# One row-sum matmul set for two attention heads, with the weights folded to 64 rows by DMA

## The chip, the cores and the metric

The kernel runs on one core of one Trainium2 chip. The metric is the device time of one execution in microseconds (us). Three executions of the kernel before took 1892.85, 1893.73 and 1894.67 us; the median, 1893.73 us, is the time that the change is measured against.

## The reference

The output is a gated mix of two blocks that read the same input `x` (2048 tokens of 1024 numbers, all in float32):

```python
g = sigmoid((x * gate_w).sum(-1, keepdims=True))
a = mha(x, wqkv, wo)             # 32 heads of 32 dimensions
b = peer(x, w_q, k1, k2, u, v)   # per token and head: best of 64 experts, gelu, weighted sum
out = g * a + (1 - g) * b

# inside mha, for each head:
scores = q @ k.T * 32 ** -0.5    # 2048 x 2048
p = softmax(scores, axis=-1)
o = p @ v                        # 2048 x 32
```

The change touches the denominators of the softmax. The kernel keeps the exponentials unnormalised, multiplies them with `v`, sums them over the keys, and divides at the end.

## The kernel before

**Stages.** First come the projections to `q` and `k`, the router of the experts, and the values `v`, stored to DRAM in two halves of 16 heads. Then comes the attention stage, head after head, about half of the time, and last the multiplication with `wo` and the output.

**Value stage.** `values(ts, half)` (L550) computes token tiles of 128 rows, 24 matmuls each, into one PSUM bank per tile. `bank()` (L99) hands out eight banks in turn, and `values_out` (L561) copies a bank to SBUF on ACT and stores it. The last four tiles of the first half are computed together (`fin0`, L626), with the weights' inner index as the outer loop, so that the weights of the second half can take their places one after the other. Then the first four tiles of the second half are computed in the same way, in banks 0 to 3, because L637 rounds the counter up to a multiple of eight. Just before `fin0` runs the tile of tokens 11, and before that `peer_turn` (L604), whose four copies on ACT each wait for a store from one shared buffer.

**Attention stage.** The 2048 x 2048 weights of a head are made transposed: keys on the 128 partitions, queries along the free dimension. One head has 16 key tiles `kt`. The loop at L875 takes two key tiles per turn; I call this a pair, and a head has pairs 0 to 7. In a turn TensorE (PE) first computes eight score matmuls of this pair (L714), each into one of the seven banks of `ring`. ScalarE (ACT) turns them into exponentials `P` of 128 x 2048 numbers per key tile (L724). Then PE multiplies the exponentials of the pair before with the values (`pv`, L735, four matmuls side by side on 32 columns each). Then the turn issues what `at(step, ...)` has put down for its two steps (a step is one key tile; a head has 16). On PE, ACT, VectorE (DVE) and the DMA queues everything runs in the order in which it is issued here.

**Row sums.** The 16 tiles `P` of a head have to be summed over all keys. `presum` (L752) splits this: tile 1 is written straight into a tile `accd`; tiles 3, 8 and 12 are added to `accd` by DMAs on the GpSimd (POOL) queue that add to what is there; each of these waits for the one before, since all three write `accd`. The other tiles are added on DVE into `acc`. At step 5 of the next head `merge` (L765) adds `accd` to `acc` on DVE; at step 8 `head_sums` (L768) takes one bank of the ring and multiplies the 128 x 2048 result with a 128 x 32 tile of ones, four matmuls side by side (L748). I call these four a set. ACT copies the bank out (`norm_sums`, L781, tile `ssb`), and the SyncE (SP) queue stores one row of every 32 to DRAM (`smd`). For every four heads, `load_r` and `norm_r` (steps 10 and 14 of the next head) load the sums, take reciprocals, multiply with the gate and store them.

**Buffers.** `P` has eight slots (pool `pp`, L661), used in turn by the 15 tiles of a head that are not `accd`. So the slot of tile 3 comes back at tile 11 of the same head, that of tile 8 at tile 0 of the next head, and that of tile 12 at tile 5 of the next head. A slot is free when both `pv` and the adder (DVE or the DMA) have read it. `acc` and `accd` have two buffers each. `finish` (L774, step 0 of the next head) copies the head's output out on ACT and stores it (`od`), and right behind it in SP's order (step 2) stand the seven loads of K and Q of the head after (`load_head`, 1.5 MB), and at step 7 a load of values (`V`).

**Loads for the end.** `wo` (4 MB) lies in one tile `wo_raw`, loaded in 16 pieces at step 11 of heads 8 to 23. `v_raw`, `AT`, the first chunk of outputs and its reciprocals follow in heads 28 to 31.

Of the kernel before, what the change touches and what calls it, by code (L numbers as in the profile page):

```python
# [30 lines left out]
def gated_mha_peer_kernel(ctx, tc, xT, wqkv, wv, wo, wq, k12, ug, v, out):  # L31
# [29 lines left out]
    nc.vector.memset(ones, 1.0)  # L61
    G64 = const.tile([128, 64], F32, name="G64")
# [3 lines left out]
    const.tile([128, 56], F32, name="fill")  # L66
# [553 lines left out]
    for t in range(4, NT - 4):  # L620
        values_out(*values([t], 0))
        if t == 5:
            Ahl = peer_act()
        if t == 10:
            peer_turn(Ahl)
    fin0 = values(list(range(NT - 4, NT)), 0)  # L626
# [10 lines left out]
    bank_no[0] += -bank_no[0] % 8  # L637
# [16 lines left out]
    wo_raw = keep.tile([128, KC, D], F32, name="wo_raw")  # L654
# [90 lines left out]
    def rowsum(ps, *srcs):  # L745
        for src in srcs:
            for qc in range(NQ):
                yield nc.tensor.matmul(ps[32 * qc:32 * qc + 32, :], ones,  # L748
                                       src[:, qc * 512:(qc + 1) * 512],
                                       start=(src is srcs[0]), stop=(src is srcs[-1]))  # L750
# [17 lines left out]
    def head_sums(h):  # L768
        i, = ring_banks(1)
        for ins in rowsum(ring[:, i, :], ACC.pop(h)):  # L770
            on_ring(ins, i)
        on_ring(norm_sums(h, ring[:, i, :]), i)
# [8 lines left out]
    def norm_sums(h, ps):  # L781
        g, j = divmod(h, 4)
        o = wk.tile([128, 512], F32, name="ssb")
        ins = nc.scalar.activation(o, ps, AF.Copy)
        dma(SMD[g][j:j + 1, :].rearrange("o (q s) -> (o q) s", q=NQ), o[::32, :])
        return ins
# [36 lines left out]
    def split_first(step):  # L823
        o = OC[0][:, 0, :]
        if step == 0:
            W0.append(zp.tile([128, 2, D], F32R, name="z1"))
            OH[0] = zp.tile([128, KC, W], F32R, name="z0")
            OL[0] = wk.tile([128, KC, W], F32R, name="acc")
            nc.vector.tensor_mul(o, o, RB[0][:, 0, :])
        elif step == 1:  # L830
            nc.scalar.activation(W0[0][:, 0], wo_raw[:, 0, :], AF.Copy)
        elif step == 2:
            nc.scalar.activation(OH[0][:, 0, :], o, AF.Copy)
        else:
            for lo, src, hi in ((W0[0][:, 1], wo_raw[:, 0, :], W0[0][:, 0]),
                                (OL[0][:, 0, :], o, OH[0][:, 0, :])):
                nc.vector.tensor_tensor(out=lo, in0=src, in1=hi.bitcast(F32), op=OP.subtract)
# [6 lines left out]
    for h in range(H):  # L844
        base = h * NT
        g, j = divmod(h, 4)
        if h < H - 1:
            at(base + NT, finish, h)
            at(base + NT + 5, merge, h)
            at(base + NT + 8, head_sums, h)  # L850
        if j == 3 and g + 1 < G:
            at(base + NT + 10, load_r, g)
            at(base + NT + 14, norm_r, g)
# [7 lines left out]
    for k in range(2 * KC):  # L861
        c = slice(k * D // 2, (k + 1) * D // 2)
        at((8 + k) * NT + 11, dma, wo_raw.rearrange("p k m -> p (k m)")[:, c], wo[:, c])
# [85 lines left out]
    def split_hi(kc):  # L949
        nc.scalar.activation(woh[kc], wo_raw[:, kc, :], AF.Copy)  # L950
# [5 lines left out]
    def split_lo(kc):  # L956
        nc.vector.tensor_tensor(out=wol[kc], in0=wo_raw[:, kc, :],
# [25 lines left out]
    split(woh[0], wol[0], wo_raw[:, 0, :])  # L983
# [67 lines left out]
```

## Time and profile before

| what | value |
|---|---|
| median of three executions | 1893.73 us (1892.85 to 1894.67) |
| the profiled execution | 1894.6 us, of which the span from the first to the last instruction is 1892.8 us |
| granted TensorE clock, mean | 0.998 |
| PE, ACT, DVE busy | 1875.8, 1158.7, 1202.2 us |
| attention stage | from about 667 to 1695 us of the span |
| DMA | 302.72 MB, mean 160 GB/s |

A line of the page's groups gives line, engine, operation, tiles (out<-in), shapes and count, then the busy time in us, the mean of one in ns, the idle time of the engine just before them, and what ended it. In a timeline the columns are start, duration, engine, line, operation, tiles and count; in brackets stands the idle time before the first, and what ended it. PEld is the loading of weights, SPq a DMA issued by SyncE. In a table by windows the columns are the window, its length, the busy time of PE, PEld, DVE, ACT and POOL with the number of instructions, the granted clock, the DMA engines' share and GB/s. A matmul's duration is its latency; matmuls overlap, so their spacing is read from the starts.

### The profile page before, as it was taken

How to read it: one execution, taken by the hardware profiler on the slowest of the kernel's cores; microseconds unless marked ns; L12 is line 12 of the kernel's file. 1: busy time of each engine (PE TensorE's matmuls, PEld its weight loads, DVE VectorE, ACT ScalarE, POOL GpSimd, SP SyncE). 2: the span in 40 equal slices, each digit the busy share in tenths (PEclk: the TensorE clock that was granted, in tenths of full speed). 3: DMA queues.
4: the chain of work that ended last, by engine and by line, in shares of the span. 5: the costliest groups of instructions: out<-in, count | busy, mean ns of one | idle time of the engine just before them, and what ended most of it. 6: DMA issues, size and time to landing. Idle time of an engine off the chain costs nothing.

```text
span 1892.8 us, 25742 instructions
## 1 busy us (share of the span) xinstructions
PE 1875.8 (99%) x10271; PEld 1157.9 (61%) x10271; DVE 1202.2 (64%) x916; ACT 1158.7 (61%) x1413; POOL 148.6 (8%) x183
## 2 busy tenths in 40 slices
PE   9999999999998999999999999999999999999999
PEld 7877777887887844444444444444444444448887
DVE  4522224866520068888888888888888888895220
ACT  4211111200121189999999999999999999993110
POOL 0000000035200000000000000000000000010000
PEclk9999999999999999999999999999999999999999
DMA  5777774420222167777777776877777777756521
GB/s 211 278 270 254 264 271 137 137 73 2 79 88 79 46 161 166 160 172 159 175 169 183 167 184 157 184 162 184 170 176 170 164 166 179 188 128 172 154 89 67
DMA packets 108082, 302.72 MB, mean 160 GB/s; under 512 B 14724, under 2 KB 48660, under 8 KB 84472
## 3 DMA queue, kind: packets, MB, share of 16 engines
q1 hardware_dynamic: 70520, 154.76, 27.4%
q0 software_dynamic: 14976, 103.29, 26.3%
q10 hardware_dynamic: 22464, 43.00, 7.0%
q8 instruction: 81, 1.33, 0.3%
q14 instruction: 41, 0.34, 0.1%
HBM read 138.73 MB, written 62.66 MB: 106 GB/s over the span
## 4 chain that ended last, share of the span: by engine, by line
PE 76%; ACT 0%; DMA 0%; ACTq 0%; issue 0%; DVE 0%
PE ring L714 28%; PE o L735 25%; PE pa L918 9%; PE bk L558 9%; PE bk L401 2%; PE ring L748 1%; PE pa L927 1%; PE o L558 0%; ACT P L724 0%; PE o L748 0%; ACT vo L564 0%; DMA vd<-vo 0%; PE bk L608 0%; ACT accd L724 0%; ACTq L71 0%
## 5 line engine op out<-in xcount | busy, mean ns | idle before, releaser
L724 ACT ACTIVATE P<-ring 128x512 f32<-128x512 f32 (+2 forms) x1034 | 914.5, 984 | 14.9 <-PE o L735 1.4
L763 DVE TENSOR_TENSOR acc<-acc,P 128x2048 f32<-128x2048 f32 x319 | 730.9, 2291 | 74.1 <-ACT P L724 48.8
L735 PE MATMUL o<-P,V 128*32 128x512 f32 x3840 | 464.8, 599 | 0.0
L714 PE MATMUL ring<-z,z 98*128 98x512 f32 x1024 | 272.0, 407 | 1.3 <-ACT P L724 0.8
L714 PE MATMUL ring<-Q,K 98*128 98x512 f32 x1024 | 272.0, 407 | 0.9 <-ACT P L724 0.9
L714 PEld LDWEIGHTS ring<-Q,K 98*128 98x128 f32 x1024 | 182.0, 188 | 145.1 <-ACT P L724 75.1
L714 PEld LDWEIGHTS ring<-z,z 98*128 98x128 f32 x1024 | 182.1, 188 | 144.1 <-ACT P L724 75.1
L735 PEld LDWEIGHTS o<-P,V 128*32 128x32 f32 x3840 | 98.8, 109 | 223.2 <-issue 214.1
L89 ACT ACTIVATE hi<-bk 128x512 fp32r<-128x512 f32 x64 | 37.6, 598 | 242.6 <-PE bk L325 226.9
L325 PE MATMUL bk<-xh,whi 128*128 128x512 f32 x448 | 176.2, 393 | 0.1
L325 PE MATMUL bk<-xh,wlo 128*128 128x512 f32 x448 | 174.4, 389 | 0.0
L325 PE MATMUL bk<-xl,whi 128*128 128x512 f32 x448 | 174.4, 389 | 0.0
L757 POOL DMA_DIRECT2D accd<-P x95 | 81.5, 858 | 1104.8 <-ACT P L724 521.4
L90 DVE TENSOR_TENSOR lo<-bk,hi 128x512 fp32r<-128x512 f32 x64 | 44.1, 689 | 187.5 <-ACT hi L89 183.0
L761 DVE TENSOR_TENSOR acc<-P 128x2048 f32<-128x2048 f32 x32 | 73.4, 2293 | 77.2 <-ACT P L724 77.2
L558 PE MATMUL bk<-wvh,xh 128*128 128x512 f32 x248 | 97.6, 393 | 4.9 <-ACT vo L564 4.9
L325 PEld LDWEIGHTS bk<-xh,whi 128*128 128x128 f32 x448 | 84.1, 188 | 24.1 <-issue 6.7
L558 PE MATMUL bk<-wvl,xh 128*128 128x512 f32 x248 | 97.0, 391 | 0.0
L558 PE MATMUL bk<-wvh,xl 128*128 128x512 f32 x248 | 97.0, 391 | 0.0
L325 PEld LDWEIGHTS bk<-xh,wlo 128*128 128x128 f32 x448 | 84.1, 188 | 17.8
L325 PEld LDWEIGHTS bk<-xl,whi 128*128 128x128 f32 x448 | 84.1, 188 | 16.9
L564 ACT ACTIVATE vo<-bk 128x512 f32<-128x512 f32 x31 | 18.5, 597 | 115.6 <-PE bk L558 109.7
(163 smaller groups left out, 1662.4 us busy)
## 6 DMA issues: line engine op xcount, KB each, us to landing
accd<-P POOLq DMA_DIRECT2D x95, 1024.0 KB, 7.5
wqt<-in_wq SPq DMA_DIRECT2D x32, 1024.0 KB
vd<-vo ACTq DMA_DIRECT2D x32, 256.0 KB
z<-kdh SPq DMA_DIRECT2D x32, 256.0 KB
z<-qdh SPq DMA_DIRECT2D x32, 256.0 KB
V<-vd SPq DMA_DIRECT2D x32, 256.0 KB
K<-kdh SPq DMA_DIRECT2D x32, 256.0 KB
Q<-qdh SPq DMA_DIRECT2D x32, 256.0 KB
```

Source lines behind the costliest of these rows:

```text
L89: nc.scalar.activation(hi, src, AF.Copy)
L90: (on or nc.vector).tensor_tensor(out=lo, in0=src, in1=hi.bitcast(F32), op=OP.subtract)
L325: nc.tensor.matmul(ps, a[:, kc, :], b[:, kc, n * 512:(n + 1) * 512], start=first, stop=last)
L401: nc.tensor.matmul(ps, a[:, kc, tok], b, start=first, stop=last)
L558: nc.tensor.matmul(p, a[:, kc, tok], b, start=first, stop=last)
L714: on_ring(nc.tensor.matmul(ring[:, i, :], K[:98, kt * 128:(kt + 1) * 128], Q[:98, qc * 512:(qc + 1) * 512], start=True, stop=True), i)
L724: on_ring(nc.scalar.activation(P[h, kt][:, q0 * 512:(q0 + m) * 512].rearrange("p (a m) -> p a m", a=m), ring[:, i:i + m, :], AF.Exp, scale ...
L735: nc.tensor.matmul(O[h][32 * qc:32 * qc + 32, :], Vt[g][:, kt, 32 * j:32 * j + 32], p[:, qc * 512:(qc + 1) * 512], start=(kt == 0), stop=( ...
L757: nc.gpsimd.dma_start(ACCD[h], P[h, kt], accum_op=OP.add)
L761: nc.vector.tensor_add(ACC[h], P[h, 0], P[h, kt])
L763: nc.vector.tensor_add(ACC[h], ACC[h], P[h, kt])
L918: nc.tensor.matmul(pa[tt, half], a[:, kc, tt * 128:(tt + 1) * 128], b[:, half * 512:(half + 1) * 512], start=(first and kc == kcs[0] and i ...
```

## The change

- **One set for two heads.** A second weight tile `ones2` has ones in rows 0 to 63 of columns 0 to 15 and in rows 64 to 127 of columns 16 to 31, zeros elsewhere. A tile `T` of 128 x 2048 holds the even head's weights in its upper 64 rows and the odd head's in its lower 64. One set gives the sums of both heads.
- **Folding.** For an even head, DVE adds `acc` and `accd` into `T`, and a DMA on the POOL queue adds the lower 64 rows of `T` to the upper ones. For an odd head, DVE adds the upper 64 rows of `accd` to those of `acc`, then writes the sum of the lower rows to the lower half of `T`, and a DMA adds the upper rows of `acc` to it. Both stand at step 5 of the next head, where `merge` stood.
- **When.** The common set stands at step 15 of the head after the odd one, for heads 0 to 29 (15 sets for 30 heads). Heads 30 and 31 stay as they were. `norm_sums` issues one store for each head. `load_r` and `norm_r` move from steps 10 and 14 to 18 and 22 after the group's last head, that is, to steps 2 and 6 of the head after the next; at step 2 `load_r` is issued ahead of `load_head`.
- **wo.** `wo_raw` becomes two tiles of 2 MB. `T` is the first half of the second one. The first tile is loaded in heads 8 to 15 as before; the four 512 KB pieces of the second are loaded at step 15 of head 30 and steps 3, 6 and 9 of head 31. `v_raw`, `AT`, the first chunk and its reciprocals move one to two heads ahead.
- **Value banks.** The counter is now set to bank 4 ahead of `fin0`, and is no longer rounded behind it: `fin0` takes banks 4 to 7, and the second half's first four tiles take 0 to 3 as before.

```diff
+    ones2 = const.tile([128, 32], F32, name="ones2")
+    nc.vector.memset(ones2, 0.0)
+    for i in range(2):
+        nc.vector.memset(ones2[64 * i:64 * i + 64, 16 * i:16 * i + 16], 1.0)
-    const.tile([128, 56], F32, name="fill")
+    const.tile([128, 24], F32, name="fill")
...
+    bank_no[0] += (4 - bank_no[0]) % 8
     fin0 = values(list(range(NT - 4, NT)), 0)
...
     values_out(*fin0)
-    bank_no[0] += -bank_no[0] % 8
     values_out(*values(list(range(4)), 1))
...
-    wo_raw = keep.tile([128, KC, D], F32, name="wo_raw")
+    wo_raw = [keep.tile([128, KC // 2, D], F32, name=f"wo_raw{i}") for i in range(2)]
+
+    T = wo_raw[1].rearrange("p k m -> p (k m)")[:, :S]
...
+    up, low = slice(0, 64), slice(64, 128)
+
+    def fold_even(h):
+        nc.vector.tensor_add(T, ACC.pop(h), ACCD[h])
+        nc.gpsimd.dma_start(T[up], T[low], accum_op=OP.add)
+
+    def fold_odd(h):
+        acc = ACC.pop(h)
+        nc.vector.tensor_add(acc[up], acc[up], ACCD[h][up])
+        nc.vector.tensor_add(T[low], acc[low], ACCD[h][low])
+        nc.gpsimd.dma_start(T[low], acc[up], accum_op=OP.add)
+
-    def head_sums(h):
+    def head_sums(h, heads=1):
         i, = ring_banks(1)
-        for ins in rowsum(ring[:, i, :], ACC.pop(h)):
+        for ins in rowsum(ring[:, i, :], T if heads == 2 else ACC.pop(h),
+                          ones=ones2 if heads == 2 else ones):
             on_ring(ins, i)
-        on_ring(norm_sums(h, ring[:, i, :]), i)
+        on_ring(norm_sums(h, ring[:, i, :], heads), i)
...
-        dma(SMD[g][j:j + 1, :].rearrange("o (q s) -> (o q) s", q=NQ), o[::32, :])
+        for i in range(heads):
+            dma(SMD[g][j + i:j + i + 1, :].rearrange("o (q s) -> (o q) s", q=NQ), o[16 * i::32, :])
...
-            at(base + NT + 5, merge, h)
-            at(base + NT + 8, head_sums, h)
+            if h == H - 2:
+                at(base + NT + 5, merge, h)
+                at(base + NT + 8, head_sums, h)
+            else:
+                at(base + NT + 5, (fold_even, fold_odd)[h % 2], h)
+            if h % 2 and h < H - 2:
+                at(base + NT + 15, head_sums, h - 1, 2)
         if j == 3 and g + 1 < G:
-            at(base + NT + 10, load_r, g)
-            at(base + NT + 14, norm_r, g)
+            at(base + NT + 18, load_r, g)
+            at(base + NT + 22, norm_r, g)
...
+    def load_wo(kc, half=slice(0, D)):
+        dma(wo_raw[kc // 4][:, kc % 4, half], wo[:, kc * D:(kc + 1) * D][:, half])
+
+    for k in range(KC):
+        at((8 + k) * NT + 11, load_wo, k // 2, slice(k % 2 * D // 2, (k % 2 + 1) * D // 2))
     for i in range(2):
-        at(28 * NT + 6 + i, dma, v_raw[64 * i:64 * i + 64, :], v)
-        at(28 * NT + 13 + 10 * i, dma, AT[:, i * S // 2:(i + 1) * S // 2],
-           ATD[:, i * S // 2:(i + 1) * S // 2])
-    at(29 * NT + 13, load_o, 0, 0, 4)
-    at(30 * NT + 7, load_o, 0, 4, KC - 1)
-    at(30 * NT + 13, load_rb, 0, 0, KC - 1, range(2))
-    at((H - 1) * NT + 2, load_rb, 0, 0, KC - 1, range(2, 4))
+        at((26 + i) * NT + 13, dma, v_raw[64 * i:64 * i + 64, :], v)
+        c = slice(i * S // 2, (i + 1) * S // 2)
+        at(28 * NT + 7 + 6 * i, dma, AT[:, c], ATD[:, c])
+        at(29 * NT + 7 + 6 * i, load_o, 0, 4 * i, 4 + 3 * i)
+        at(30 * NT + 7 + 6 * i, load_rb, 0, 0, KC - 1, range(2 * i, 2 * i + 2))
+    for i, step in enumerate((15, 19, 22, 25)):
+        at(30 * NT + step, load_wo, 4 + i)
```

More of the change, by code (lines that the diff above doesn't have):

```diff
@@ L743, in gated_mha_peer_kernel, with rowsum @@
     SUMS = (1, 3, 8, 12), (2, 4, 6)
-    def rowsum(ps, *srcs):
+    def rowsum(ps, *srcs, ones=ones):
         for src in srcs:
@@ L778, in finish, with norm_sums @@
         dma(OD[g][32 * j:32 * j + 32, :].rearrange("d (q s) -> q d s", q=NQ), o)
-    def norm_sums(h, ps):
+    def norm_sums(h, ps, heads=1):
         g, j = divmod(h, 4)
@@ L830, in split_first @@
         elif step == 1:
-            nc.scalar.activation(W0[0][:, 0], wo_raw[:, 0, :], AF.Copy)
+            nc.scalar.activation(W0[0][:, 0], wo_raw[0][:, 0, :], AF.Copy)
         elif step == 2:
@@ L834, in split_first @@
         else:
-            for lo, src, hi in ((W0[0][:, 1], wo_raw[:, 0, :], W0[0][:, 0]),
+            for lo, src, hi in ((W0[0][:, 1], wo_raw[0][:, 0, :], W0[0][:, 0]),
                                 (OL[0][:, 0, :], o, OH[0][:, 0, :])):
@@ L949, in split_hi @@
     def split_hi(kc):
-        nc.scalar.activation(woh[kc], wo_raw[:, kc, :], AF.Copy)
+        nc.scalar.activation(woh[kc], wo_raw[kc // 4][:, kc % 4, :], AF.Copy)
         if kc < KC - 1:
@@ L956, in split_lo @@
     def split_lo(kc):
-        nc.vector.tensor_tensor(out=wol[kc], in0=wo_raw[:, kc, :],
+        nc.vector.tensor_tensor(out=wol[kc], in0=wo_raw[kc // 4][:, kc % 4, :],
                                 in1=woh[kc].bitcast(F32), op=OP.subtract)
@@ L982, in gated_mha_peer_kernel @@
         wo_mm(pa, 0, [kc], False, False)
-    split(woh[0], wol[0], wo_raw[:, 0, :])
+    split(woh[0], wol[0], wo_raw[0][:, 0, :])
     ps_odd = Pool("ps_odd", space=PSUM)
```

3 lines of the change are left out of this document (removed).

## The prediction

> **What bounds the kernel now.** I read the page's busy times and chain first, then the groups, then the attention stage by windows and by timeline.
>
> ```profile
> PE 1875.8 (99%) x10271; PEld 1157.9 (61%) x10271; DVE 1202.2 (64%) x916; ACT 1158.7 (61%) x1413; POOL 148.6 (8%) x183
> ...
> PE ring L714 28%; PE o L735 25%; PE pa L918 9%; PE bk L558 9%; PE bk L401 2%; PE ring L748 1%; PE pa L927 1%; PE o L558 0%; ACT P L724 0%; PE o L748 0%; ACT vo L564 0%; DMA vd<-vo 0%; PE bk L608 0%; ACT accd L724 0%; ACTq L71 0%
> ...
> L763 DVE TENSOR_TENSOR acc<-acc,P 128x2048 f32<-128x2048 f32 x319 | 730.9, 2291 | 74.1 <-ACT P L724 48.8
> ```
>
> ```profile
> 677.00:1670.00 993.00, 992.32 (x6186) 462.55 (x6184) 849.12 (x385) 965.98 (x1123) 79.15 (x93) 1.00 0.75 171
> ```
>
> PE never rests in the attention stage (992.32 of 993.00 us), and the chain goes through its score and value matmuls. ACT follows at 965.98, DVE at 849.12, the DMA engines at 0.75. So PE's work there is worth its full price, as long as the near rivals do not step forward. Head 12 on PE shows the price:
>
> ```profile
> 1063.43 2.11 PE L714 MATMUL ring<-z,z 98*128 98x512 f32 x8
> ...
> 1067.32 2.14 PE L714 MATMUL ring<-z,z 98*128 98x512 f32 x8
> ...
> 1071.13 1.04 PE L748 MATMUL ring<-acc,ones 128*32 128x512 f32 x8
> 1072.10 2.12 PE L714 MATMUL ring<-z,z 98*128 98x512 f32 x8
> ```
>
> A plain pair takes 1067.32 - 1063.43 = 3.89 us; the pair with the set takes 1072.10 - 1067.32 = 4.78. A set costs 0.89 us of PE, not its rows' 1.04.
>
> **The wait that has almost no margin.** The slot of tile 3 is given free by a DMA and taken by ACT for tile 11.
>
> ```profile
> 1060.67 0.86 POOL L757 DMA_DIRECT2D accd<-P  x1 [9.22 <-PE ring L714]
> 1074.68 0.86 POOL L757 DMA_DIRECT2D accd<-P  x1 [13.15 <-DMA accd<-P]
> 1082.75 0.86 POOL L757 DMA_DIRECT2D accd<-P  x1 [7.21 <-ACT P L724]
> ```
>
> ```profile
> 1073.34 2.37 ACT L724 ACTIVATE P<-ring 128x1536 f32<-128x1536 f32 x2
> ```
>
> ```profile
> L724 ACT ACTIVATE P<-ring 128x1024 f32<-128x1024 f32 x394 | 387.0, 1054 | 0.7 <-DMA accd<-P 0.7
> ```
>
> Tile 3's DMA starts at 1060.67 and its landing lets tile 8's start at 1074.68. ACT's two exponentials end at 1075.71; the second has 1024 columns, so tile 11 begins near 1075.71 - 1.05 = 1074.66. Head 15 shows what happens when the slot is late:
>
> ```profile
> 1168.40 2.11 PE L714 MATMUL ring<-Q,K 98*128 98x512 f32 x8
> 1172.30 0.96 PE L714 MATMUL ring<-Q,K 98*128 98x512 f32 x3
> 1173.94 1.48 PE L714 MATMUL ring<-Q,K 98*128 98x512 f32 x5 [0.68 <-ACT P L724]
> 1177.21 2.11 PE L714 MATMUL ring<-Q,K 98*128 98x512 f32 x8
> ```
>
> ```profile
> 1172.44 3.78 ACT L724 ACTIVATE P<-ring 128x1536 f32<-128x1536 f32 x4 [1.35 <-PE o L735]
> 1172.89 0.86 POOL L757 DMA_DIRECT2D accd<-P  x1 [15.05 <-DMA accd<-P]
> ```
>
> ACT resumes at 1172.44, 0.45 us before POOL's next issue; both wait for that landing. So in head 12 the slot was free at 1074.68 - 0.45 = 1074.23, a margin of 0.4 us. In head 15 tile 11 began 1172.44 - 1168.40 = 4.04 us after its pair, in head 12 1074.66 - 1072.10 = 2.56: 1.48 late. PE's next pair took 1177.21 - 1172.30 = 4.91, 1.02 longer than 3.89: the ring hides about 0.45 us of such a delay and PE pays the rest.
>
> **The change part by part.**
>
> *Sets.* 31 sets in the ring become 16. 15 x 0.89 = -13.3 us. This is on the path. The 15 copies out of the bank go too, 15 x 0.60 us of ACT by `ssb`:
>
> ```profile
> L784 ACT ACTIVATE ssb<-ring 128x512 f32<-128x512 f32 x31 | 18.6, 599 | 12.9 <-PE ring L748 12.9
> ```
>
> ACT stays behind PE (966 - 9 of 993 - 13): nothing for that.
>
> *The slot of tile 3.* Today the set stands at step 8, between tiles 3 and 11, and gives the DMA 0.89 us. Moved to step 15, it no longer does. If the landing stays where it is, ACT comes to tile 11 0.89 us earlier and waits 0.89 - 0.4 = 0.5 us; 0.45 of that is hidden. A typical head pays 0.05 us, one with a late landing up to 0.89. The view of L757 counts who waited for these DMAs, and their times from issue to landing:
>
> ```profile
>   ACT P L724: 0.7, 3
> ...
> DMA to landing us min/median/max: 6.8/7.5/15.4
> ```
>
> So three waits of 95 were over the pipeline's own gap; head 15's was the longest transfer. The subtraction that I did for head 12 gives margins from none (heads 7, 14, 15, 18) to 0.7 us in the others; PE's share averages some 0.15 us, and 30 heads give +4.5. Ends: 0 (all hidden) and 30 x 0.89 = +27 (nothing hidden). I take 4.5, being nearest to head 12's rows.
>
> *Does the landing stay?* Its 13.5 us are mostly the seven loads of K and Q, which SP issues before:
>
> ```profile
> 1056.74 0.53 SPq L71 DMA_DIRECT2D od<-osb  x1
> 1057.37 1.53 SPq L71 DMA_DIRECT2D K<-kdh  x2
> ...
> 1064.03 0.39 SPq L71 DMA_DIRECT2D V<-vd  x1
> 1072.86 0.52 SPq L71 DMA_DIRECT2D smd<-ssb  x1
> 1075.08 0.35 SPq L71 DMA_DIRECT2D rr<-smd  x1
> ```
>
> In seven heads `load_r` (0.35 us) now stands ahead of these loads; in 15 heads the set's copy on ACT runs at the head's start, so that `od` comes about 0.1 us later. `smd` is issued some 4 us before `od`, and `rr` needs 1075.08 - 1072.86 = 2.2 us behind it, so that wait is over in time. The store `rd<-rr` now waits at step 6 for DVE, with the V load behind it on SP; V is for the next group of heads. The fold's DMA is queued behind tile 3's. Averaged, I take 0.13 us a head: 30 x 0.13 = +4. Ends: -2, if the DMA engines freed of half of `wo`'s pieces in heads 16 to 23 help, and the slower rival's +12.5.
>
> *The folds.* DVE gains one addition for each odd head, 15 x 2.29 = 34 us: 849 + 34 = 883 of about 985, hidden; DVE's tiles are read long before their slots come back. POOL gains 30 issues of 0.86 us, behind DVE's fold:
>
> ```profile
> 1064.52 2.28 DVE L766 TENSOR_TENSOR acc<-acc,accd 128x2048 f32<-128x2048 f32 x1
> ```
>
> It ends at 1066.80, for an odd head at 1069.1; tile 8's DMA, next in POOL's order, waits for 1074.68 anyway. The transfer:
>
> ```profile
> q0 software_dynamic: 14976, 103.29, 26.3%
> q10 hardware_dynamic: 22464, 43.00, 7.0%
> ```
>
> ```profile
> 1065.20:1074.20 9.00, 9.00 (x62) 3.99 (x64) 8.69 (x5) 8.47 (x10) 0.00 (x0) 1.00 0.77 178
> 1074.20:1076.20 2.00, 2.00 (x18) 0.56 (x18) 1.99 (x1) 2.00 (x3) 0.86 (x1) 1.00 0.11 27
> 1076.20:1081.90 5.70, 5.70 (x32) 3.07 (x31) 5.40 (x3) 5.49 (x7) 0.00 (x0) 1.00 1.02 211
> ```
>
> 0.263 x 1892.8 / 103.29 = 4.8 us of all engines per MB, so 2.5 us for a fold's 0.52 MB. Idle before tile 8's transfer are 9.00 x 0.23 + 2.00 x 0.89 = 3.9 us. It fits: nothing. The set needs the fold 10 steps (19 us) later.
>
> *A rule that speaks against this.* The Trainium skill (SBUF — State Buffer, section "Door 1: The DMA port swizzle") says that a transfer on partitions 0 to 63 reaches only 8 of 16 ports and has half the bandwidth. By it a fold would last as long as a full transfer, twice the 2.5 us. No adding DMA of 64 rows is in this trace, so nothing here shows it. Against it speaks that adding transfers (4.8 us per MB) are slower than the plain ones of q10 (0.07 x 1892.8 / 43.00 = 3.1), so that ports are not what limits them on 128 rows. The slower rival below has a price from rows alone.
>
> *Value banks.* PE's one long wait in the value stage goes:
>
> ```profile
> 573.34 0.39 PE L558 MATMUL bk<-wvh,xl 128*128 128x512 f32 x1
> 578.61 0.79 PE L558 MATMUL bk<-wvh,xh 128*128 128x512 f32 x1 [4.88 <-ACT vo L564]
> ```
>
> ```profile
> 577.96 0.60 ACT L564 ACTIVATE vo<-bk 128x512 f32<-128x512 f32 x1 [0.40 <-DMA vd<-vo]
> ```
>
> ```profile
> 578.60:582.20 3.60, 3.59 (x9) 2.86 (x10) 0.00 (x0) 0.00 (x0) 0.00 (x0) 0.55 0.34 127
> ```
>
> It ends with the fourth copy (578.56), so `fin0`'s fourth tile holds bank 0, `fin0` has banks 5, 6, 7, 0, and token tile 11 before it bank 4. The wait costs 4.88 us, and 3.6 us at a clock of 0.55 cost 3.6 x 0.45 = 1.6 more: -6.5. But `fin0` now begins in bank 4, right behind tile 11:
>
> ```profile
> 551.81 0.39 PE L558 MATMUL bk<-wvh,xh 128*128 128x512 f32 x1
> ```
>
> ```profile
> 554.28 0.60 ACT L611 ACTIVATE at<-bk 128x512 fp32r<-128x512 f32 x1 [2.21 <-DMA atd<-at]
> 554.78 0.59 ACT L564 ACTIVATE vo<-bk 128x512 f32<-128x512 f32 x1
> ```
>
> That bank's copy ends at 555.37, behind the four `at` copies, while PE is there at 551.81: a new wait of 3.6 us, and likely the clock's 1.6: +5.2. Sum -1.3; -2.9 if the clock holds.
>
> *The rest.* `wo`'s last 2 MB load beside head 31's two adding DMAs: +0.5 (0 to 1.5). `ones2` costs DVE three small memsets while the first loads are on their way: nothing. DVE, POOL and ACT keep their order at the head's start.
>
> **Sum.** -13.3 + 4.5 + 4 - 1.3 + 0.5 = -5.6 us, against the profiled execution's 1894.6 us; that lies 0.9 above the median of 1893.73, so 1888.1 us.
>
> **Rivals.**
>
> *Slower: the folds push tile 8's DMA.* If a fold holds an engine for 5 us, tile 8's transfer lands 2.5 us later. It lands now near 1082.75 - 0.45 = 1082.3, and the next head's tile 0 takes its slot near 1084.4: a margin of 2.1, and 1.2 in the odd heads, where the set no longer stands in between. Late by 0.4 (hidden) and 1.3 (0.85 paid): 15 x 0.85 = 12.8, so 1888.1 + 12.8 = 1900.9. For it: the skill's rule; DMA is at 0.75 and rises. Against: the idle 3.9 us. It decides once the push is over 2 us. The same end is reached if tile 3 lands 0.6 us later in all heads, since then all further delay is paid, 3 us for each 0.1.
>
> *No change: the slot eats the sets.* If tile 3 lands 0.3 us later instead of 0.13, +5 more: 1893. For it: margins of 0.4 in an untouched head.
>
> *All hidden.* Landings come no later and ACT's waits vanish in the ring: -13.3 - 1.3, 1879. Against: heads 7, 14, 15 and 18.
>
> **How the numbers follow.** The forecast (1881 to 1890) has 0.47, all hidden 0.04, no change (1890 to 1897.5) 0.26, slower 0.23. A measurement tells about 0.2%, 3.8 us, from no change. So faster 0.51, same 0.26, slower 0.23. The range runs from 1881, below the forecast, to 1902, just above the slower rival; the forecast's own is 1881 to 1890.
>
> **What the next profile would show.** L748 in the ring with 128 matmuls instead of 248, and plain pairs of 3.89 us. ACT `P` idle on DMA `accd`: 0.3 to 0.6 us in most heads, summing to 10 to 25 us, PE's share 5 to 10. The 4.88 us wait gone, and a new one of 3.6 us near 552. I am wrong if tile 3's DMA lands more than 0.3 us later after its head's start, if tile 8's makes ACT wait at a head's start, or if PE waits for a fold.

## The result and the profile after

Four executions of the changed kernel took 1917.33 to 1925.31 us, median 1920.25; the kernel before had a median of 1893.47 us beside them. The ratio is 1.0143 (95% interval 1.0120 to 1.0167): the change makes the kernel about 27 us slower. The prediction was 1888.1 us, with 1902 as its upper end.

The page of the kernel after: busy times, queue 0 (the queue of all adding DMAs, folds included), the chain by engine and by line, and the group of the exponentials.

```profile
PE 1883.0 (98%) x10151; PEld 1154.4 (60%) x10151; DVE 1238.3 (65%) x934; ACT 1146.7 (60%) x1398; POOL 173.9 (9%) x213
...
q0 software_dynamic: 17376, 119.02, 30.3%
...
PE 45%; DMA 16%; issue 7%; ACT 6%; DVE 3%; ACTq 0%; DVEq 0%; POOLq 0%
...
L731 ACT ACTIVATE P<-ring 128x512 f32<-128x512 f32 (+2 forms) x1033 | 909.9, 991 | 56.4 <-DMA accd<-P 33.5
```

Before, the chain was made of PE's matmuls. Now DMA has 16% of it and ACT 6%, and ACT's exponentials (L731, before L724) were idle for 33.5 us because of the DMAs that add to `accd`; before, that was 0.7.

The attention stage in the same window as before, by engine:

```profile
677.00:1670.00 993.00, 976.92 (x5954) 448.11 (x5956) 866.62 (x393) 937.29 (x1087) 102.73 (x121) 1.00 0.82 182
```

PE got 5954 matmuls through in the window where it had done 6186, and rested for 16 us of it. The DMA share rose from 0.75 to 0.82.

The sets themselves went as planned. The groups of L755 (before L748), by lines:

```profile
L755 PE MATMUL ring<-wo_raw,ones 128*32 128x512 f32 x120 | 15.6, 592 | 0.0
...
L755 PE MATMUL ring<-acc,ones 128*32 128x512 f32 x8 | 1.0, 592 | 0.0
```

These are 128 matmuls, 16 sets, in place of 248 and 31. To see what came in their place, the stage is worked out from the starts of the score matmuls in each trace: the time from the first pair to the last, less 255 pairs of 3.90 us, less 0.88 us for each set. What is left, "waits", is PE's loss to waits and to a slower clock in the one execution that was traced. "Tile 3 lands" is the median over heads 1 to 30, counted from the head's first score; "half clock" is the time in the stage at a granted clock of 0.5.

```
                     sets  first to last pair  waits  tile 3 lands  half clock
before                 31        1023.98         2.2      22.55         0
after                  16        1046.57        38.0      23.54        10.2
```

The sets gave 15 x 0.88 = 13.2 us, and the waits took 36 us. 35.4 of the 38.0 us lie in pair 6 of the heads, the pair whose scores stand behind ACT's wait for the slot of tile 3. Head 12, which the prediction showed of before, shows it; first PE, then ACT, then POOL on the timeline of the kernel after:

```profile
1072.54 2.11 PE L721 MATMUL ring<-z,z 98*128 98x512 f32 x8
...
1076.43 2.14 PE L721 MATMUL ring<-z,z 98*128 98x512 f32 x8
...
1080.36 0.96 PE L721 MATMUL ring<-z,z 98*128 98x512 f32 x3
1081.83 0.73 PE L721 MATMUL ring<-z,z 98*128 98x512 f32 x2 [0.51 <-ACT P L731]
1082.74 0.99 PE L721 MATMUL ring<-z,z 98*128 98x512 f32 x3 [0.18 <-ACT P L731]
...
1085.52 2.12 PE L721 MATMUL ring<-z,z 98*128 98x512 f32 x8
```

```profile
1080.75 7.45 ACT L731 ACTIVATE P<-ring 128x1024 f32<-128x1024 f32 x8 [1.61 <-DMA accd<-P]
```

```profile
1065.93 0.85 POOL L764 DMA_DIRECT2D accd<-P  x1 [7.38 <-ACT P L731]
1074.67 0.82 POOL L786 DMA_DIRECT2D wo_raw<-acc  x1 [7.88 <-DVE wo_raw L785]
1081.18 0.90 POOL L764 DMA_DIRECT2D accd<-P  x1 [5.69 <-DMA accd<-P]
```

Tile 3's DMA is issued at 1065.93 and has landed when ACT goes on at 1080.75, 14.8 us later; the prediction's subtraction for head 12 of before gives 1074.23 - 1060.67 = 13.6. ACT waits 1.61 us. The pairs before run at 3.89 us (1076.43 - 1072.54), and pair 6 takes 1085.52 - 1080.36 = 5.16: PE pays 1.26. Between tile 3's issue and tile 8's stands the fold of the odd head before (1074.67). In before, ACT waited in three heads; the waits of after are in 26:

```profile
ACT P L731 <- DMA accd<-P: 33.5, 26, 2.8
```

The median of heads 1 to 30 loses 1.1 us. In 22 of these 30 heads PE loses in pair 6, within 0.05 us, just the time by which tile 3 lands later than 22.5 us into the head. The prediction's numbers give that bound: in head 12, whose first score starts at 1051.71, tile 11 begins at 1074.66 - 1051.71 = 22.95; less the 0.89 of the set, plus the 0.45 that the ring hides, that is 22.5.

Heads 28 and 30, whose loads for the end run beside tile 3's DMA, lose 3.7 and 5.5, and the granted clock has a part in these. Head 30 on PE, and then windows of after, with the clock in the third column from the right:

```profile
1674.13 1.22 PE L721 MATMUL ring<-z,z 98*128 98x512 f32 x2 [2.08 <-ACT P L731]
```

```profile
554.50:561.30 6.80, 5.49 (x13) 4.33 (x14) 0.00 (x0) 1.08 (x2) 0.00 (x0) 0.50 0.22 80
1605.80:1609.20 3.40, 3.33 (x15) 1.27 (x19) 3.19 (x3) 3.40 (x6) 0.00 (x0) 0.50 1.12 254
1674.10:1680.90 6.80, 6.77 (x23) 2.77 (x24) 6.49 (x4) 4.14 (x5) 0.00 (x0) 0.50 0.93 172
```

The first window is in the value stage. In the two heads PE ran at half the clock for 3.4 and 6.8 us, which is about 5 of the 9.2 us that they lose.

The value stage shows the predicted exchange of one wait for another. PE and ACT of after:

```profile
551.98 0.39 PE L563 MATMUL bk<-wvh,xl 128*128 128x512 f32 x1
555.81 0.79 PE L563 MATMUL bk<-wvh,xh 128*128 128x512 f32 x1 [3.44 <-ACT vo L569]
```

```profile
554.67 0.60 ACT L616 ACTIVATE at<-bk 128x512 fp32r<-128x512 f32 x1 [2.20 <-DMA atd<-at]
555.17 0.59 ACT L569 ACTIVATE vo<-bk 128x512 f32<-128x512 f32 x1
```

The wait of 4.88 us is gone and one of 3.44 us stands where the prediction put it. The first attention pair starts at 667.30, at the same time as before (667.32). This agreement alone shows little: in the traces of the experiments below, kernels with this same value stage start the pair anywhere from 662.6 to 668.0. A part of that is the clock. The same wait of 3.4 us goes with 6.83 us at half the clock here, with 3.41 in another of these traces (folds left out) and with none in a third (half folds).

### The profile page after: what moved, and what is told of

Read it like the earlier page. It is cut to its first block, busy times and chain, and to the rows that moved or that the text cites. A ratio compares the mean times of both kernels' runs of the same rounds, so it can differ in the third digit from the quotient of the medians.

```text
span 1915.6 us, 25488 instructions
## 1 busy us (share of the span) xinstructions
PE 1883.0 (98%) x10151; PEld 1154.4 (60%) x10151; DVE 1238.3 (65%) x934; ACT 1146.7 (60%) x1398; POOL 173.9 (9%) x213
## 3 DMA queue, kind: packets, MB, share of 16 engines
q0 software_dynamic: 17376, 119.02, 30.3%
## 4 chain that ended last, share of the span: by engine, by line
PE 45%; DMA 16%; issue 7%; ACT 6%; DVE 3%; ACTq 0%; DVEq 0%; POOLq 0%
DMA accd<-P 15%; PE ring L721 12%; PE o L742 11%; PE pa L948 9%; PE bk L563 9%; ACT P L731 5%; PE bk L406 2%; DVE acc L770 2%; PE pa L957 1%; ACT accd L731 1%; PE ring L755 1%; DVE wo_raw L785 0%; DVE acc L784 0%; DMA atd<-at 0%; PE o L563 0%
## 5 line engine op out<-in xcount | busy, mean ns | idle before, releaser
L731 ACT ACTIVATE P<-ring 128x512 f32<-128x512 f32 (+2 forms) x1033 | 909.9, 991 | 56.4 <-DMA accd<-P 33.5
L721 PE MATMUL ring<-z,z 98*128 98x512 f32 x1024 | 280.2, 412 | 10.7 <-ACT P L731 10.0
L721 PE MATMUL ring<-Q,K 98*128 98x512 f32 x1024 | 279.3, 410 | 9.0 <-ACT P L731 8.9
```

Of the source, the lines that this page charges most:

```text
L721: on_ring(nc.tensor.matmul(ring[:, i, :], K[:98, kt * 128:(kt + 1) * 128], Q[:98, qc * 512:(qc + 1) * 512], start=True, stop=True), i)
L731: on_ring(nc.scalar.activation(P[h, kt][:, q0 * 512:(q0 + m) * 512].rearrange("p (a m) -> p a m", a=m), ring[:, i:i + m, :], AF.Exp, scale ...
```

## The experiments

All times are medians; each ratio is against the kernel before on the same chip, with its 95% interval. The medians of the kernel before lie between 1892.8 and 1894.1 us in these comparisons, so a difference between two experiments holds to a microsecond or two.

**The theories.** The first, *loop*: in a head the transfers of tile 3, tile 8, tile 12 and K and Q form a closed row that is already nearly as long as the head, so that bytes put anywhere in it lengthen each head. The second, *neighbour*: the fold hurts only because it is in flight beside tile 3's transfer, whose landing has no margin. The third, *slot*: the folds matter little, and the loss is the 0.89 us which the moved set no longer gives to tile 3.

**Folds left out.** The common set of this kernel sums stale rows.

```diff
     def fold_even(h):
         nc.vector.tensor_add(T, ACC.pop(h), ACCD[h])
-        nc.gpsimd.dma_start(T[up], T[low], accum_op=OP.add)
...
         nc.vector.tensor_add(T[low], acc[low], ACCD[h][low])
-        nc.gpsimd.dma_start(T[low], acc[up], accum_op=OP.add)
```

> The changed kernel without the 30 adding DMAs of the folds; DVE's additions, the moved set and all moved loads stay (the row sums of heads 0 to 29 are then not complete). Theory A: the folds' 0.5 MB lengthen the chain of adding DMAs (tile 3, 8, 12, then the next head's K and Q, then tile 3), so that tile 3 lands about 0.8 us later in its head. Without them it lands near 22.6 us again and the time falls to about 1888 us (1884 to 1893). Theory B: the moved set and the moved loads alone make tile 3 late. Then the landing stays near 23.4 us and the time at 1912 us or more.

Measured: 1894.25 us, ratio 0.9998 (0.9988 to 1.0008). The 30 DMAs cost 1920.25 - 1894.25 = 26 us, so the slot theory doesn't account for the loss by itself. But the rest of the change is no gain either: its sets' 13.2 us are eaten too. Tile 3 lands at 22.68, the waits sum to 18.0 us, 10 of them in pair 6. Another 4.1 us are lost in the first pairs of heads 7, 27 and 29, where ACT waits 2.07 us for tile 8's DMA. ACT still waits often in this trace:

```profile
ACT P L731 <- DMA accd<-P: 26.2, 35, 2.1
```

**The set alone moved.** The kernel before, with its one set for each head at step 15.

```diff
-            at(base + NT + 8, head_sums, h)
+            at(base + NT + (8 if h == H - 2 else 15), head_sums, h)
...
-            at(base + NT + 10, load_r, g)
-            at(base + NT + 14, norm_r, g)
+            at(base + NT + 18, load_r, g)
+            at(base + NT + 22, norm_r, g)
```

> The kernel before with one set for each head as before, but at step 15 instead of step 8 (reciprocals at steps 2 and 6 of the head after); nothing else. It takes 0.89 us from between tiles 3 and 11 and saves nothing. Theory A (the prediction's term for the slot): about +4.5 us, 1898 us (1894 to 1902), tile 3 landing near 22.6 us. Theory B: tile 3 lands later too, because later loads on the SyncE queue are no longer held back by the sums' store at step 8; then 1905 us or more.

Measured: 1903.2 us, ratio 1.0048 (1.0029 to 1.0066), so +9 us (5.5 to 12.5) for the slot of tile 3 alone. That is between the two expectations; the median landing, 22.62 against 22.55 before, speaks for theory A, with twice its size. No work is added or removed here; the same set merely stands behind tile 11 instead of in front of it. 11.8 of its 13.0 us of waits are in pair 6.

**Half of each fold.** The changed kernel, folding 32 of the 64 rows (the other 32 are left out of the sums).

```diff
+    up2, low2 = slice(0, 32), slice(64, 96)
...
-        nc.gpsimd.dma_start(T[up], T[low], accum_op=OP.add)
+        nc.gpsimd.dma_start(T[up2], T[low2], accum_op=OP.add)
...
-        nc.gpsimd.dma_start(T[low], acc[up], accum_op=OP.add)
+        nc.gpsimd.dma_start(T[low2], acc[up2], accum_op=OP.add)
```

> The changed kernel with each fold's DMA cut to 32 of its 64 rows (the row sums of heads 0 to 29 then lack some keys). Without folds the time was 1894, with them 1920. Theory A1, the folds cost by their bytes on the DMA engines: half of the 26 us, about 1907 us (1902 to 1912). Theory A2, they cost by being issued and completed, whatever their size: 1916 us or more.

Measured: 1900.46 us, ratio 1.0036 (1.0021 to 1.0050). That is below both expectations: half the bytes cost 6 us, the other half 20. Tile 3 lands at 22.85. The cost is not in proportion to bytes, as it would be if the DMA engines were the bound.

**Folds later.** The changed kernel with its folds at step 10, behind tile 8's DMA in POOL's order. The common set has to follow, to step 8 of the next odd head, where it gives that head's tile 3 its 0.89 us again. The four last loads of `wo` change their order too, because `T` is in use for longer.

```diff
-                at(base + NT + 5, (fold_even, fold_odd)[h % 2], h)
+                at(base + NT + 10, (fold_even, fold_odd)[h % 2], h)
...
-                at(base + NT + 15, head_sums, h - 1, 2)
+                at(base + NT + 24, head_sums, h - 1, 2)
...
-            at(base + NT + 18, load_r, g)
-            at(base + NT + 22, norm_r, g)
+            at(base + NT + 28, load_r, g)
+            at(base + NT + 32, norm_r, g)
...
-    for i, step in enumerate((15, 19, 22, 25)):
-        at(30 * NT + step, load_wo, 4 + i)
+    for kc, step in ((6, 15), (7, 19), (4, 25), (5, 26)):
+        at(30 * NT + step, load_wo, kc)
```

> The changed kernel with its fold moved from step 5 of the next head to step 10, where POOL issues it behind tile 8's DMA (that one waits for the two adds of tiles 4 to 7); the common set, load_r and norm_r move back by 9 to 10 steps with it (the set to step 8 of the odd head's successor), and four wo pieces change places. The loop theory says that it doesn't matter where in the head the fold's 0.5 MB stands, because tile 3's, tile 8's and tile 12's DMAs and the loads between them already fill the head: the fold now stands ahead of tile 12's DMA, that one lands later, the next K and Q loads with it, and the time stays near the changed kernel's 1920, not under 1905. The neighbour theory says that only a fold in flight beside tile 3's and tile 8's DMAs is harmful: then the fold is nearly free here, the slot gets back the set's 0.89 us in half of the heads, and the time is 1885 to 1894, as without folds.

Measured: 1889.53 us, ratio 0.9978 (0.9968 to 0.9987). POOL's order in this kernel, with tile 3's issue at 1311.39, tile 8's at 1325.45, the fold at 1329.64 and tile 12's at 1332.82:

```profile
1311.39 0.85 POOL L764 DMA_DIRECT2D accd<-P  x1 [9.26 <-ACT P L731]
1325.45 0.85 POOL L764 DMA_DIRECT2D accd<-P  x1 [13.21 <-DMA accd<-P]
1329.64 0.82 POOL L786 DMA_DIRECT2D wo_raw<-acc  x1 [3.35 <-DVE wo_raw L785]
1332.82 0.90 POOL L764 DMA_DIRECT2D accd<-P  x1 [2.36 <-ACT P L731]
```

The same bytes move (queue 0 carries 119.02 MB in both), and by the medians of its landing events tile 12's DMA is no earlier than in the changed kernel: 7.3 us into the next head, against 6.7. By the loop theory the time had to stay near 1920. It fell by 31 us, so that theory falls.

**Folds later, and left out.** The same kernel without its fold DMAs (its common set sums stale rows).

> The kernel with late folds, its 30 fold DMAs left out and nothing else changed (each common set then sums one head's sums twice or stale rows, so the output is not the reference's). What is left of a fold's cost at its late place is the difference: if a fold behind tile 8's DMA is free, the time stays at 1888 to 1891; if it still delays the next tile 3's DMA by the 0.2 to 0.4 us that even heads wait longer here than without folds, the time is 1883 to 1887; in both cases the fold's early place alone cost some 20 us.

Measured: 1889.31 us, ratio 0.9975 (0.9963 to 0.9986). Behind tile 8's DMA a fold costs nothing that can be measured; in front of it, it costs 26 us. So the neighbour theory stands. The remaining difference between the two schedules without folds, 1894.25 - 1889.31 = 5 us, is what the set's new step (and the steps of `load_r` and `norm_r`) gives back. In this trace most odd heads lose less than 0.1 us; most even heads, which have no set in front of tile 11, still lose 0.4 to 0.9.

**How a fold that is issued behind tile 3's DMA can delay it.** In the trace's packets of queue 0, counted in each head from tile 3's issue on, tile 3's DMA is 128 packets of 0.63 us each and a fold 64. The medians over heads 1 to 30, in us from the head's first score:

```
                        before   folds left out   after   folds late
fold issued                -            -         16.9       26.1
packet 100 of queue 0    18.56        18.71       18.77      18.78
packet 128 of queue 0    22.02        22.17       20.68      22.30
tile 3's DMA landed      22.55        22.68       23.54      22.87
packets by then            128          128         179        128
```

In the changed kernel the queue has moved as many packets as tile 3 has by 20.68, earlier than before, but 51 of the fold's 64 packets are over before tile 3's last one. So "issued behind" is not "moved behind": the last packets of tile 3 end 0.9 us later. Whether a fold's packets are mixed with tile 3's on each DMA engine, or run on the engines that are through while the slowest of them is held up, is not told by these packets, which don't name the engine. The semaphore of each landing gives a hint, since it goes up in 16 steps. Without folds the 11th step of tile 3's DMA is at 20.08 and the last four are at 21.46, 21.90, 22.45 and 22.68; with folds the 11th is at 20.12 and the last four at 22.10, 22.48, 23.25 and 23.54, and the fold's own first step comes at 22.79 (medians). So only those parts of the transfer are delayed that were late without a fold too, and this speaks for the second; why they are slowed isn't shown.

**K and Q behind tile 3.** The prediction put most of tile 3's 13.5 us down to the seven loads of K and Q. Three kernels move these loads to POOL's queue, right behind tile 3's DMA: the kernel before, the changed kernel without folds, and the changed kernel.

```diff
-            at(base + 2, load_head, h + 1)
+            at(base + 4, load_head, h + 1, nc.gpsimd)
```

> The kernel before with the same move of the K and Q loads. PE is the bound there and waits for hardly any slot, so both theories expect 1892 to 1895 us; if the move itself helped or hurt (GpSimd's issues, a K or Q that comes late), it would show here.

Measured on the kernel before: 1893.03 us, ratio 0.9996 (0.9987 to 1.0006). Tile 3 lands at 17.83 instead of 22.55, so the loads were what made it slow; and the time doesn't move, because there the set covers the slot.

> The changed kernel without its 30 fold DMAs (so each common set sums one head's sums twice or stale rows, and the output is not the reference's), and with the K and Q loads on POOL's queue behind tile 3's DMA, which lets tile 3 land at about 18 us of its head. The slot theory says that without folds the sets' 13 us are lost at the wait for tile 3 alone: with that wait gone the time is 1880 (1877 to 1884). If the sets' time was not on the path at all, it stays at 1890 or above.

Measured on the kernel without folds: 1887.06 us, ratio 0.9963 (0.9951 to 0.9976); 1880 was expected, and neither 1880 nor "1890 or above" came. In 26 of the heads 1 to 30 PE loses less than 0.1 us, as the slot theory has it. But heads 12, 14, 28 and 30 lose 1.3, 3.8, 1.5 and 1.2 us: there tile 3 lands at 23.6 to 24.7 again. All four are among the heads with further loads (`wo` in heads 8 to 15, `AT` and the reciprocals in 28 to 30); what delays it there stays open.

> The changed kernel with the seven loads of the next head's K and Q issued on the GpSimd queue at step 4, behind tile 3's adding DMA, instead of on the SyncE queue ahead of it. Theory A (the order of the transfers makes tile 3 late): tile 3 lands some 8 us after its issue, near 17 us of its head, its slot is never waited for, and the sets' 13 us come through: about 1880 us (1877 to 1885). Theory C (the DMA engines as a whole have no room for the folds, in whatever order): tile 8 or 12 is late instead, and the time stays above 1900 us.

Measured on the changed kernel: 1960.15 us, ratio 1.0342 (1.0325 to 1.0360), far off the expectation. In this kernel POOL issues the fold in every head 0.57 us after tile 3 has landed, so the fold is no longer beside that transfer; but tile 3 itself lands at 22.97, not near 17, and the common set on PE waits for the fold. The view of the fold's line:

```profile
its engine sat idle before it (us, times) until:
  DMA accd<-P: 79.4, 11
  DVE acc L770: 33.9, 4
who waited for it (us, times):
  PE ring L755: 23.2, 11
...
DMA to landing us min/median/max: 9.7/10.6/12.0
```

Of the 82.8 us of waits 33 lie in pair 6 and 33 in pair 7, where the set stands. The attention stage has 13 stretches at half the clock, 61.4 us in all, so up to some 30 us of the loss are clock. Why tile 3 comes this late stays open.

> The kernel with late folds, and beside it the K and Q loads on POOL's queue behind tile 3's DMA, and the value banks without the rounding. In this order POOL's DMAs are tile 3, K and Q, tile 8, fold, tile 12, each behind the other. If all of them fit in a head of about 32 us (the transfers of the kernel before with this order ended with 5 us to spare at the slot), the sets' 13 us and the banks' 5 both come through: 1875, 1871 to 1882. If the row of transfers is longer than the head, tiles 8 or 12 come late instead and the time is over 1893.

Measured with late folds, K and Q on POOL's queue, and no bank rounding: 1899.61 us, ratio 1.0033 (1.0022 to 1.0044). The expectation of 1875 was missed. The waits are 29.7 us, 10.9 of them in pair 6 and 12.8 in pair 4, where the kernels above lose under 1. The page's row of queue 0, which now carries K and Q as well:

```profile
q0 software_dynamic: 26976, 166.72, 44.7%
```

That is 44.7% of all engines' time on one queue, in POOL's order, against 31.3% with late folds alone. It doesn't fit; which transfer is the first to be late stays open.

**K and Q at a later step of SP's queue.**

```diff
-            at(base + 2, load_head, h + 1)
+            at(base + 7, load_head, h + 1)
```

> The changed kernel with one edit: its K and Q loads stand at step 7 instead of 2 (the fold stays at step 5). If the fold's harm is only that it runs beside the last packets of tile 3's transfer, that transfer is now over before the fold is issued (at 15 to 18 us), and the time falls from 1920 to 1881 to 1888. If the fold's bytes hurt wherever they stand among tile 3's, tile 8's and the loads, the time stays above 1895.

> The kernel with late folds and without bank rounding (1886.4 against 1893.5), with the seven K and Q loads moved from step 2 to step 7 on SP's own queue, so that tile 3's DMA, issued at about 9 us of the head, has the engines to itself for its 5 us and the loads follow beside it. If the wait for tile 3 is all that still eats the sets, tile 3 lands at 15 to 18 us, tile 8 and the fold still fit, and the time falls by the 9 to 12 us of waits that are left: 1876 (1873 to 1880). If the loads, tile 8's DMA and the fold then crowd each other as they did behind each other on POOL's queue, tile 8 or K and Q come late and the time is 1890 or above.

Measured: 1920.02 us, ratio 1.0142 (1.0123 to 1.0161), on the changed kernel, and 1886.49, ratio 0.9958 (0.9942 to 0.9975), with late folds and no bank rounding. Both miss, for one reason: the edit does almost nothing. SP had nothing to wait for between its steps 2 and 7, so it issues the loads as early as before. SP in head 20 of the first of these kernels, whose first score starts at 1322.59:

```profile
1327.61 0.54 SPq L76 DMA_DIRECT2D od<-osb  x1
1328.25 0.95 SPq L76 DMA_DIRECT2D K<-kdh  x2
...
1335.05 0.39 SPq L76 DMA_DIRECT2D V<-vd  x1
```

K is issued 5.7 us after that; in the changed kernel, with step 2, it is 1324.38 - 1318.70 = 5.7 too:

```profile
1323.73 0.54 SPq L76 DMA_DIRECT2D od<-osb  x1
1324.38 0.88 SPq L76 DMA_DIRECT2D K<-kdh  x2
```

Only in every fourth head (5, 9, 13 and so on), where another wait of SP holds the loads back, does tile 3 land at 16 to 17.5 us. The fold is issued at 15.3 in these heads, beside the same transfer, and costs pair 6 nothing: with a margin the neighbour is harmless. But PE loses 1.0 to 1.9 us at that head's end instead, and PE's waits now name the loads:

```profile
PE ring L721 <- DMA z<-shd: 4.5, 3, 1.7
PE ring L721 <- DMA z<-qdh: 4.2, 3, 1.8
```

**Value banks.** The kernel before with the bank counter set to 4 ahead of `fin0`, as in the change; and the kernel before with its rounding line simply taken out.

```diff
+    bank_no[0] += (4 - bank_no[0]) % 8
     fin0 = values(list(range(NT - 4, NT)), 0)
...
-    bank_no[0] += -bank_no[0] % 8
```

> The kernel before with the new numbering of the value banks alone. The prediction's term: a wait of 3.6 us in front of the last four tiles of the first half replaces the one of 4.9 us behind them, -1.3 us, 1892.2 us (1890.5 to 1894). If the old wait simply went: -6.5 us, 1887.

Measured: 1893.56 us, ratio 0.9996 (0.9986 to 1.0005): nothing that can be measured.

> The kernel before without the line that rounds the bank counter, so that the last four tiles of the first half have banks 5, 6, 7, 0 and the next four 1 to 4. No two neighbours share a bank: both waits should be gone, -6.5 us, 1887 us (1885.5 to 1889). If something else held PE there, between -4 and 0.

Measured without any rounding: 1888.55 us, ratio 0.9971 (0.9961 to 0.9981), about 5.5 us faster. In its list of PE's waits the long wait of the value stage is missing; only a short one is left:

```profile
PE o L558 <- ACT vo L564: 0.7, 1, 0.7
```

> The changed kernel with the K and Q loads behind tile 3's DMA and without any rounding of the value banks (5, 6, 7, 0 and then 1 to 4). Under theory A 5 to 6 us below the same kernel with bank 4, about 1875 us (1871 to 1880), faster than the kernel before and the one without rounding. Under theory C above 1895 us.

Measured, with the rounding taken out of the slow kernel with K and Q on POOL's queue: 1947.21 us, ratio 1.0280 (1.0263 to 1.0297), 13 us below the same kernel with it. The banks' part of this is 5 to 6 by the run above; what the rest is stays open.

**Both gains together.** Late folds and no rounding.

> The kernel with late folds (1889.5 against 1893.0) and without the line that rounds the bank number, as in the kernel before without rounding, which was 5.5 us faster. The value banks lie 180 us ahead of the first fold, so the two gains should add: 1884 (1882 to 1887). If the bank line's gain came from something that the rings' order in the attention stage decides (bank numbers run on into it), it does not carry over and the time stays at 1888 to 1891.

Measured: 1886.40 us, ratio 0.9963 (0.9950 to 0.9976). This is below the kernel before by its interval, and far below the changed one. It is 3 us under the late folds alone, where 5.5 was to be had, and its interval overlaps that of the rounding line alone (0.9961 to 0.9981), so it is not shown that the common sets add anything to that line.

The stage as above, for the kernels that carry the argument:

```
                                  sets  first to last pair  waits  tile 3 lands
set alone moved to step 15          31        1034.82        13.0      22.62
change, folds left out              16        1026.53        18.0      22.68
change, half folds                  16        1031.95        23.4      22.85
change                              16        1046.57        38.0      23.54
change, folds late                  16        1020.03        11.5      22.87
the same, folds left out            16        1021.94        13.4      22.80
no folds, K and Q behind tile 3     16        1019.79        11.2      19.35
```

## Why the prediction was wrong

- **"Sets", -13.3.** Right: 15 x 0.88 = -13.2 us, in the trace of the change and in all its variants.
- **"The slot of tile 3", +4.5 between 0 and +27.** Right in its mechanism and its place (pair 6), and half the size: the set moved alone cost 9 us. The prediction took the landings of the kernel before. Summed over heads 1 to 30, what they exceed 22.5 us by is 5.6 us, near its 4.5; in the trace with the set moved it is 10.5, because ten landings come after 23.0 there, against four before. Why they do isn't shown.
- **"Does the landing stay?", +4 by 0.13 us a head.** For all parts but the folds the 0.13 was right, to the hundredth by luck: without folds tile 3 lands at 22.68 against 22.55. The step that failed is its sentence on the fold, "is queued behind tile 3's", which puts the fold's effect on tile 3 at nothing: with the folds the landing moves by 0.99 us, not 0.13.
- **"The folds ... It fits: nothing."** Wrong, and the dearest step: 26 us. The idle stretch ahead of tile 8's transfer was there, and a fold takes about the engine time that was reckoned: queue 0 took 0.303 x 1915.6 - 0.263 x 1892.8 = 82.6 us of all engines more for 15.7 MB more, 5.25 us per MB, so 2.75 us for a fold against the 2.5 of the prediction. But the sum of idle time was no cover, since the fold was issued some 6 us before tile 3 landed and 51 of its 64 packets went ahead of tile 3's last. Half folds delay tile 3's median landing by 22.85 - 22.68 = 0.17 us and cost 6, whole ones by 0.86 and cost 26. Why twice the bytes delay it five times as much isn't shown.
- **The slower rival** named tile 8's transfer as the place; that was not it, for no head of the changed kernel loses time in its first pair to that transfer (three heads of the kernel without folds do). Its last sentence was: the same end, if tile 3 lands later in all heads, "3 us for each 0.1". By that price 0.99 us instead of the 0.6 that it set at 1900.9 gives 1900.9 + 3.9 x 3 = 1912.6, and the slot's 4.5 us that were missing give 1917, against 1920 measured. The price was right, about 1 us per head for each 1 us of landing, and the delay was thought unlikely.
- **The rule that speaks against the change** (the Trainium skill, SBUF — State Buffer, "Door 1: The DMA port swizzle": half of the bandwidth for 64 rows). It is not seen here: 5.25 us per MB for the folds beside 4.8 for the transfers of 128 rows, where half the bandwidth would make it 9.6, if the ports were what limits the transfers of 128 rows; and the fold's packets take 0.63 us each as the others do. The slower end came, but not by this rule.
- **"Value banks", -1.3.** The wait came where it was put, 3.44 us for 3.6. But PE then ran at half the clock until 561.30, not for 3.6 us but for 561.30 - 555.81 = 5.5: 3.44 + 2.7 = 6.1 in place of 6.5, which is nearly nothing, as the run of its own says. How much the clock adds differs between the traces of this value stage (6.83, 3.41 or 0 us at half clock), so the 5.5 is this trace's.
- **"The rest", +0.5.** Not isolated. Without folds, sets (-13.2), slot (+9) and banks (0) leave 4 us to account for until the measured 0. The trace of that kernel has two losses of this size: the 4.1 us at the starts of heads 7, 27 and 29, and 1.6 us in the first head, at half the clock. The trace of the changed kernel has neither, so what the 4 us are stays open.

The sum then reads -13.2 for the sets, +9 for the slot, +26 for the folds, 0 for the banks and about +4 for the rest: +26, against the 26.8 between the two medians. The +4 is only what the other parts leave over, so the agreement is no test; sets, slot, folds and banks have runs or traces of their own.

## What to carry to other kernels

A transfer that has to land on time isn't protected by being issued first: what is issued beside it before it lands can delay its last packets, and idle engine time later on doesn't count as cover. So look for the next issue behind a landing that has no margin, and put extra transfers behind that landing; here five steps turned a loss of 26 us into nothing. And before an instruction is taken out of the bound engine's order, ask which wait it was covering: 0.89 us of PE in front of a slot with 0.4 us of margin were worth most of what their removal saved.

## What the runs showed of the hardware

- The granted clock goes by steps of 3.41 us. All stretches at 0.5 in these traces last one, two or (once) three such steps, but for the one that stands at the end of each trace. They also start on a fixed grid: in the changed kernel 554.50, 1605.81 and 1674.08 lie 308.0 and 20.0 steps apart. The attention stage shows them right behind PE's waits of 1.36 us (head 28) and 2.08 us (head 30). But not each wait of this length has one behind it: with half folds the 3.44 us in the value stage brought none; there the grid cuts the wait into 1.88 and 1.56 us. So what a wait costs by the clock depends on where it falls. In the changed kernel with K and Q on POOL's queue such stretches were 61.4 us of the stage. The Trainium skill (TensorE: Matmul & The Clock Gate, "What's actually happening") gives the window as 3413 ns, as seen here, and says that the clock falls after at least one idle window; here some waits shorter than a window were enough.
- Two adding DMAs of one queue that don't depend on each other run at the same time: 51 of the second one's 64 packets were over before the first one's last. The Trainium skill (DMA: Bandwidth & Descriptors, "Two DMAs through the same engine are not ordered") says that nothing orders DMAs across the 16 engines. The overlap of the packets fits that; which engine moved which isn't recorded.
- A DMA's step in the program is no time: SP issued K 5.7 us into the head whether the load stood at step 2 or at step 7.
